# Attention with keys on partitions, in one written order per engine, ahead of an unchanged mixture of experts

## The chip, the cores and the metric

The kernel runs on one core of one Trainium2 chip. The metric is the device time of one execution in microseconds. A core has a matrix engine (PE, with its weight loads shown apart as PEld), a vector engine (DVE), a scalar engine (ACT), a general engine (POOL) and an engine that mostly issues transfers (SP). Each executes its own list of instructions in order, and waits on semaphores where it needs another's result. Matmul results go to PSUM, which has eight banks; all else lies in SBUF.

## The reference

Attention with a local window and some global keys, then a router that sends every token to one of eight experts. Sizes: batch B=4, heads H=8, sequence S=768, head dim D=64; `n_global` = 8, `n_local` = 96; 3,072 tokens of 512 values; F=1024. All data are float32.

```python
scores = (1/sqrt(D)) * q @ k.T
rel = pos[:, None] - pos[None, :]
is_global = pos[None, :] < n_global
is_local = (rel >= 0) & (rel < n_local)
dist = where(is_global & ~is_local, n_local, abs(rel))
scores = where(is_global | is_local, scores - slope[h] * dist, -1e9)
a = exp(scores - scores.max(-1))
x = (a / (a.sum(-1) + 1e-9)) @ v            # then (B,H,S,D) -> (B*S, H*D)
logits = x @ w_gate
e = argmax(logits); g = softmax(logits)[e]
out = g * (relu(x @ w1[e]) @ w2[e])
```

`q`, `k` and `v` are normal numbers times 0.1.

## The kernel before, in words

**Attention** (`banded`, L249 to L431). The 768 queries of a sequence are six blocks of 128, so there are 24 blocks `n`, and `i = n % 6` is a block's place in its sequence. Queries lie on partitions. A block sees its own 128 keys, the 128 before them, and 32 columns for global keys: three kinds of block, of 128 columns (`i` = 0), 288 with the global keys masked out of the middle (`i` = 1) and 288 with them (`i` >= 2). A unit is two heads of a block, so a block has four.

Per unit, `scores` (L321) does two matmuls into `sp` (each head on its own 64 rows of the array), DVE adds a bias from a table (L334) and takes the row maximum (L336), ACT takes the exponential with the maximum as bias and sums the row (L342). `weights_t` (L346) transposes the weights `p` by 128x128 on PE (L354, L357), and ACT and DVE copy them out (L359, L360, L364). `values` (L367) multiplies them with `v`: four matmuls a unit, six where the global keys stand apart, with 128 queries as the stationary side and 64 columns moving (L381). After four units DVE divides by the sums (`normalize`, L227). The unit loop (L410) runs the transposes one unit and the values two units behind the scores. `prep_q` and `prep_k` transpose the next block's raw rows (L239).

**Router.** `block_logits` (L158) transposes the block's x (L161) and multiplies with `w_gate` (L168); `choose` (L174) and `dispatch` (L196) run once a sequence, and six indirect writes on POOL (L219) put the rows into `xs_dram` by expert.

**Order.** Engines other than PE follow a scheduler's order; PE keeps the program's. Tiles come from pools whose buffers rotate. The loads of `q`, `k`, `v` are issued by SP, two blocks ahead, three of 256 KB each. The first two experts' weights (four transfers of 1 MB each, L140) are issued by SP at block 6.

**Choice of branch.** `n_global` and `n_local` are read at the start and a flag tells whether the banded branch is enough (L108 to L115); every engine loads it (L521) and branches. The other branch, `general` (L434), computes all keys and isn't run with these inputs.

**Experts** (L530 on). DVE makes a table of 31 tiles of 128 rows from the counts; POOL gathers a tile's rows (`xg`, L609); PE transposes them (`px`, L619), multiplies with `w1t` (`ph`, L633) and `w2t` (`py`, L643); SP loads the next tile's weights (L140); POOL writes the rows out (L647). Weights have two buffers.

Of the kernel before, what the change touches and what calls it, by code (L numbers as in the profile page):

```python
# [1 line left out]

# [7 lines left out]
F32 = mybir.dt.float32  # L10
# [6 lines left out]
SP = mybir.EngineType.SP  # L17


@with_exitstack  # L20
def kernel(
# [19 lines left out]
    NBLK = S // P           # query blocks of a sequence  # L41
    NPAIR = H // 2          # two heads fill the partitions with their dims
    NDC = DM // P
    NFC = F // P
    GW = 32                 # global keys that the banded branch has room for
    LW = P + 1              # and the widest window: one block and the query's own key
    WIN = 2 * P + GW
    XW = DM + 4             # a token's row: x, gate, token number, padding
    NEG = 1.0e9
    FAR = 1.0e6  # L50
    NA = E                  # first tile of every expert
    NB = NTOK // P - 1      # most tiles that can remain after those
# [9 lines left out]
    # Rows of tokens by expert: expert e has rows e * NTOK and on.  # L62
    xs_dram = dram.tile([E * NTOK, XW], I32, name="xs_dram")

# [1 line left out]
    ident = const.tile([P, P], F32, name="ident")  # L66
    masks.make_identity(nc, ident[:])
    iota_p = const.tile([P, 1], F32, name="iota_p")
    nc.gpsimd.iota(iota_p[:], pattern=[[0, 1]], base=0, channel_multiplier=1,
                   allow_small_or_imprecise_dtypes=True)  # L70
    col = const.tile([P, P], F32, name="col")
    nc.gpsimd.iota(col[:], pattern=[[1, P]], base=0, channel_multiplier=0,
                   allow_small_or_imprecise_dtypes=True)
    before = const.tile([P, P], BF16, name="before")
    nc.vector.tensor_scalar(before[:], col[:], iota_p[:, 0:1], None, ALU.is_gt)
    ones = const.tile([P, P], BF16, name="ones")
    nc.vector.memset(ones[:], 1.0)
    rev8 = const.tile([P, E], F32, name="rev8")
    nc.gpsimd.iota(rev8[:], pattern=[[-1, E]], base=E, channel_multiplier=0,
                   allow_small_or_imprecise_dtypes=True)  # L80
    ebase = const.tile([P, E], F32, name="ebase")
    nc.gpsimd.iota(ebase[:], pattern=[[NTOK, E]], base=0, channel_multiplier=0,
                   allow_small_or_imprecise_dtypes=True)
    base_e = const.tile([P, E], F32, name="base_e")
    nc.vector.tensor_copy(out=base_e[:], in_=ebase[:])
    tokid = const.tile([P, NBLK], I32, name="tokid")
    nc.gpsimd.iota(tokid[:], pattern=[[P, NBLK]], base=0, channel_multiplier=1)

    wg = const.tile([P, NDC, E], F32, name="wg")
    nc.scalar.dma_start(out=wg[:], in_=moe_w_gate.rearrange("(c p) e -> p c e", p=P))  # L90

# [1 line left out]
    words = const.tile([P, 2, 2], I32, name="words")  # L93
    nc.scalar.dma_start(out=words[:, 0, :], in_=n_global.bitcast(I32).partition_broadcast(P))
    nc.scalar.dma_start(out=words[:, 1, :], in_=n_local.bitcast(I32).partition_broadcast(P))
    part_i = const.tile([P, 3, 2], I32, name="part_i")
    nc.vector.tensor_copy(out=part_i[:, 0, :], in_=words[:, :, 1])
    nc.vector.tensor_scalar(part_i[:, 1, :], words[:, :, 0], 16, None, ALU.logical_shift_right)
    nc.vector.tensor_scalar(part_i[:, 2, :], words[:, :, 0], 0xFFFF, None, ALU.bitwise_and)
    part_f = const.tile([P, 3, 2], F32, name="part_f")  # L100
    nc.vector.tensor_copy(out=part_f[:], in_=part_i[:])
# [599 lines left out]
```

## Time and profile before

| | us |
|---|---|
| three executions | 953.45, 955.39, 968.07; median 955.39 |
| span of the profiled execution (first to last instruction) | 926.3 |
| first bias addition of attention (`z`, L334) | 24.11 |
| last value matmul of attention ends | 425.2 |
| first `ph` matmul of the experts | 455.37 |

| group, by shape | count | mean ns |
|---|---|---|
| PE `po`<-`vt,pT`, 64 columns | 704 | 316 |
| PE `pt`<-`ident,p`, 128 rows | 352 | 336 |
| PE `sp`, 288 columns | 320 | 525 |
| DVE `z`<-`sp,bias`, 576 / 256 elements | 80 / 16 | 756 / 424 |
| DVE `top`<-`z`, 576 elements | 80 | 745 |
| DVE `xr`<-`po,den`, 512 elements | 24 | 692 |
| ACT `p`<-`z,top`, 288 / 128 elements | 160 / 32 | 525 / 392 |
| ACT `qt`<-`pt`, 512 elements | 24 | 588 |
| POOL scatter `xs_dram` | 24 | 986 |
| POOL copy `kt`, 128 elements | 20 | 344 |

The profile is of one execution. A group's mean is from start to end of one instruction; matmuls overlap, so the distance from start to start is shorter than that mean. "Clock" is the share of PE's full clock that was granted in a stretch. A line of the timeline has start, length, engine, line, operation, output and inputs, rows and columns, and how many instructions of the kind are merged; square brackets give an idle time before it and what ended it.

### The profile page before, as it was taken

The numbers are of one execution on the slowest core, as the hardware profiler recorded it, in microseconds if no ns is written. First come the engines' busy times: TensorE is split into PE (matmuls) and PEld (weight loads), VectorE is DVE, ScalarE is ACT, GpSimd is POOL, SyncE is SP. The second block draws the span as 40 slices with busy tenths as digits, with TensorE's granted clock in tenths as the row PEclk, the third lists the DMA queues.
The fourth block names the chain that finished last, engine by engine and source line by source line (L and its number), as shares of the span: only waits on it lengthen the run. The fifth ranks groups of instructions, "written<-read, shape, count | busy, mean of one in ns | idle before, by whom it ended". The sixth has DMA issues, their size and how long they took to land.

```text
span 926.3 us, 12677 instructions
## 1 busy us (share of the span) xinstructions
PE 854.6 (92%) x4956; PEld 654.0 (71%) x4956; DVE 283.2 (31%) x686; ACT 213.8 (23%) x629; POOL 98.5 (11%) x135
## 2 busy tenths in 40 slices
PE   1899999999999999995399999999999999999995
PEld 1677777777878787874376867767686767667682
DVE  7743325654275548551301111111111111111100
ACT  0542324543255545541010000000000000000000
POOL 2000000200020002002311111111111111110000
PEclk9975556996599979995599999999999999999998
DMA  7753213411161113001279997898888879797870
GB/s 137 198 170 121 57 23 79 128 35 27 30 172 35 35 35 116 1 1 50 80 253 339 320 316 256 301 346 282 327 296 306 315 286 334 277 345 246 328 286 0
DMA packets 132243, 168.81 MB, mean 182 GB/s; under 512 B 79946, under 2 KB 79946, under 8 KB 132176
## 3 DMA queue, kind: packets, MB, share of 16 engines
q1 hardware_dynamic: 124480, 148.91, 48.9%
q0 software_dynamic: 6880, 18.99, 5.5%
q8 instruction: 42, 0.69, 0.3%
q14 instruction: 25, 0.20, 0.1%
q10 hardware_dynamic: 816, 0.02, 0.0%
HBM read 157.11 MB, written 14.47 MB: 185 GB/s over the span
## 4 chain that ended last, share of the span: by engine, by line
PE 74%; DMA 10%; issue 6%; DVE 5%; ACT 1%; SPq 1%; POOL 1%; POOLq 0%; DVEq 0%; ACTq 0%
PE ph L633 17%; PE po L381 17%; PE py L643 16%; DMA w1t<-in_moe_w_dram 9%; PE sp L331 7%; PE pt L354 7%; PE pl L168 3%; PE pt L239 3%; PE pt L357 2%; PE pt L161 2%; ACT p L342 1%; PE px L619 1%; SPq L140 1%; DVE bias L308 1%; DMA xs_dram<-xr,slot_i 1%
## 5 line engine op out<-in xcount | busy, mean ns | idle before, releaser
L633 PEld LDWEIGHTS ph<-xT,w1t 128*128 128x128 f32 x1984 | 229.5, 194 | 25.0 <-issue 13.8
L633 PE MATMUL ph<-xT,w1t 128*128 128x128 f32 x1984 | 231.6, 278 | 8.8 <-DMA w1t<-in_moe_w_dram 7.0
L643 PE MATMUL py<-w2t,hT 128*128 128x512 f32 x496 | 217.8, 593 | 0.0
L643 PEld LDWEIGHTS py<-w2t,hT 128*128 128x128 f32 x496 | 92.0, 190 | 104.2 <-issue 104.2
L381 PE MATMUL po<-vt,pT 128*128 128x64 f32 x704 | 126.2, 316 | 0.0
L636 ACT ACTIVATE hT<-ph 128x1024 f32<-128x1024 f32 x31 | 31.7, 1023 | 405.4 <-PE ph L633 405.4
L381 PEld LDWEIGHTS po<-vt,pT 128*128 128x128 f32 x704 | 114.7, 234 | 6.8
L342 ACT ACTIVATE p<-z,top 128x288 f32<-128x288 f32 (+1 forms) x192 | 96.5, 503 | 59.9 <-DVE top L336 47.4
L334 DVE TENSOR_TENSOR z<-sp,bias 128x576 f32<-128x576 f32 (+1 forms) x96 | 67.2, 701 | 103.7 <-PE sp L331 101.2
L354 PE MATMUL pt<-ident,p 128*128 128x128 f32 x352 | 75.3, 336 | 15.4 <-ACT p L342 14.7
L354 PEld LDWEIGHTS pt<-ident,p 128*128 128x128 f32 x352 | 44.1, 163 | 60.3 <-ACT p L342 31.7
L331 PE MATMUL sp<-kt,qt 64*128 64x288 f32 (+1 forms) x384 | 82.0, 511 | 2.0 <-DVE kt L244 2.0
L646 DVE TENSOR_SCALAR y<-py,gate 128x512 f32<-128x512 f32 x31 | 23.3, 751 | 177.2 <-PE py L643 177.2
L623 DVE TENSOR_TENSOR to<-xg,inv_i 128x1 int32<-128x1 int32 x31 | 4.9, 160 | 210.5 <-DMA out_dram<-y,to 202.8
L381 PE MATMUL po<-vt,gT 32*128 32x64 f32 x256 | 67.5, 351 | 0.0
L359 ACT COPY pT<-pt 128x256 f32<-128x256 f32 (+1 forms) x96 | 33.9, 353 | 143.1 <-PE pt L357 120.7
L336 DVE TENSOR_REDUCE top<-z 128x2 f32<-128x576 f32 (+1 forms) x96 | 66.1, 690 | 0.3
L647 POOL DMA_INDIRECT out_dram<-y,to x31 | 31.6, 1020 | 238.9 <-DVE gate L625 192.7
L381 PEld LDWEIGHTS po<-vt,gT 32*128 32x128 f32 x256 | 47.4, 230 | 11.1
L609 POOL DMA_INDIRECT xg<-xs_dram,grow x31 | 31.9, 1029 | 170.6 <-PE px L619 165.0
L331 PEld LDWEIGHTS sp<-kt,qt 64*128 64x128 f32 x384 | 34.7, 222 | 12.1 <-issue 7.6
L219 POOL DMA_INDIRECT xs_dram<-xr,slot_i x24 | 23.7, 986 | 178.4 <-DVE slot_i L216 104.6
(120 smaller groups left out, 490.7 us busy)
## 6 DMA issues: line engine op xcount, KB each, us to landing
w1t<-in_moe_w_dram SPq DMA_DIRECT2D x62, 1024.0 KB, 10.9
w2t<-in_moe_w_dram SPq DMA_DIRECT2D x62, 1024.0 KB, 7.5
raw_q<-in_q_dram SPq DMA_DIRECT2D x24, 256.0 KB, 3.1
raw_k<-in_k_dram SPq DMA_DIRECT2D x24, 256.0 KB, 3.2
vt<-in_v_dram SPq DMA_DIRECT2D x24, 256.0 KB, 4.7
xg<-xs_dram,grow POOLq DMA_INDIRECT x31, 6.1
out_dram<-y,to POOLq DMA_INDIRECT x31, 7.4
xs_dram<-xr,slot_i POOLq DMA_INDIRECT x24, 3.5
```

Source lines behind the costliest of these rows:

```text
L331: nc.tensor.matmul(sp[:, a, 0:w], lhsT=qts[n][r, m, :], rhs=kt[r, m, ds(k0, w)], start=True, stop=True, skip_group_check=True)
L334: nc.vector.tensor_tensor(z[:, :, 0:w], sp[:, :, 0:w], biases[kind][:, 2 * m:2 * m + 2, :], ALU.add)
L336: nc.vector.tensor_reduce(top[:], z[:, :, 0:w], AX.X, ALU.max, negate=True)
L342: nc.scalar.activation(p[:, a, 0:w], z[:, a, 0:w], AF.Exp, bias=top[:, a:a + 1], scale=1.0, accum_out=blk[n][:, h:h + 1])
L354: nc.tensor.transpose(pts[a][:, j, :], p[:, a, ds(j * (P + GW), P)], ident[:])
L359: nc.scalar.copy(pT[:, 0, 0:nb, :], pts[0][:, 0:nb, :])
L381: nc.tensor.matmul(po[:, h, :], lhsT=lhs, rhs=rhs, start=(j == 0), stop=(j == len(terms) - 1), skip_group_check=True)
L609: nc.gpsimd.indirect_dma_start(out=xg[j % XB][:].bitcast(I32), out_offset=None, in_=xs_dram[:], in_offset=bass.IndirectOffsetOnAxis(ap=gro ...
L633: nc.tensor.matmul(ph[:, f, :], lhsT=w1t[:, c, ts(f, P)], rhs=xT[:, c, :], start=(c == 0), stop=(c == NDC - 1), skip_group_check=True)
L636: nc.scalar.activation(hT[:], ph[:], AF.Relu)
L643: nc.tensor.matmul(py[:], lhsT=hT[:, f, :], rhs=w2t[:, f, :], start=(f == 0), stop=(f == NFC - 1))
L647: d = nc.gpsimd.indirect_dma_start(out=out[:], out_offset=bass.IndirectOffsetOnAxis(ap=fs[j]["to"][:, 0:1], axis=0), in_=y[:], in_offset=N ...
```

## The change

Attention and router are rewritten; the experts (and `general`) keep their text.

- Keys lie on partitions: a score matmul has 128 keys as the stationary side and 128 queries moving, so the exponentials come out as the values' moving side and no transpose of them is needed. A block has 16 score matmuls and 16 value matmuls (`v` with 64 columns is stationary, 128 queries move, two heads in two column halves of the array); the first block of a sequence has half of each.
- There are no columns of their own for global keys. A window is taken to be at most 97 keys, so the first 32 keys of the block before are outside it; after that block's own scores POOL overwrites them (`kg` into `kt`, `vg` into `v`) with the sequence's first 32 keys and values.
- No row maximum. The exponential is of score plus bias, in place. POOL adds the two key blocks (`both`), and matmuls with a matrix of ones and with `w_gate` (`sums`) give each query's sums and unscaled logits together; these are transposed (`tokens_u`) and divided (`normal`). The sums are kept in `den`, and at the end a flag asks that all are between 0.125 and 1e12 and that `n_global` <= 32 and 1 <= `n_local` <= 97. Otherwise `general` runs after it and does the work again. The flag is loaded by all engines after attention instead of at the start.
- All of it is recorded by `Flow`, in the order written, and played within one critical section: each engine gets its instructions in that order, and waits on semaphores of `Flow`'s own that are derived from what is read and written. At the end SP waits for every transfer. Tiles are slices of one SBUF tile and of one PSUM tile of eight banks: scores in 0 to 3, values in 4, sums in 5, x in 6, and the incoming `k` shares bank 3, the incoming `q` has 7.

The loop, and the methods that it calls, cut to their core:

```diff
+    def scores(self, n):
+        for g in range(2):
+            for mm in range(2):
+                for ab in range(2 if i else 1):
+                    kt = self.kt[(n - ab) % 3]
+                    for a in range(2):
+                        r = slice(64 * a, 64 * a + 64)
+                        m = 2 * g + mm
+                        c = 2 * P * mm + P * ab
+                        f.pe.matmul(self.psum[:, 2 * g + a, c:c + P], lhsT=kt[r, m, :], rhs=qt[r, m, :], ...)
+    def weigh(self, n, g):
+            f.dve.tensor_tensor(e, s, self.bias[:, g, :, 1:3, :]..., ALU.add)
+    def exponent(self, n, g):
+        f.act.activation(e, e, AF.Exp)
+    def both(self, n, g):
+            f.pool.tensor_tensor(self.es[n % 3][:, g], e[:, :, 0:P], e[:, :, P:2 * P], ALU.add)
+    def values(self, n, bank):
+        for m in range(4):
+            for ab in range(nb):
+                for a in range(2):
+                    r = slice(64 * a, 64 * a + 64)
+                    f.pe.matmul(po[r, m, :], lhsT=self.v[(n - ab) % 6][:, 2 * m + a, :],
+                                rhs=self.e[n % 2][:, m // 2, 2 * a + m % 2, P * ab:P * ab + P], ...)
+        return lambda: f.act.copy(self.ot[n % 2], po)
+    def sums(self, n, bank):
+        for j in range(3):
+            for m in range(4):
+                r = slice(32 * m, 32 * m + 32)
+                ...
+                f.pe.matmul(self.psum[r, bank, 0:P], lhsT=lhsT, rhs=rhs, ..., tile_position=(0, 32 * m))
+        return lambda: f.act.copy(self.us, self.psum[:, bank, 0:P])
+    def tokens_x(self, n, bank):
+        for m in range(4):
+            f.pe.transpose(self.psum[:, bank, ts(m, P)], self.ot[n % 2][:, m, :], ident)
+    def tokens_u(self, n, bank):
+        self.f.pe.transpose(self.psum[:, bank, 256:384], self.us, ident)
+    def normal(self, n, ubank):
+        f.dve.tensor_scalar(den, ut[:, :, 16:18], 1e-9, None, ALU.add)
+        f.dve.reciprocal(r, den)
+        f.dve.tensor_tensor(self.lw, ..., ALU.mult)
+        f.dve.tensor_reduce(self.lg[b % 2][:, i, :], ..., ALU.add)
+    def rows(self, n, bank):
+        f.dve.tensor_tensor(self.xr[b % 2][:, i, 0:512]..., self.psum[:, bank, :]..., self.rcp..., ALU.mult)
...
+        O, U, T0, T1, SK = 4, 5, 6, 7, 3
+        for n in range(N + 3):
+            if live:
+                at.scores(n)
+                if n + 4 < N:
+                    at.loads(n + 4)
+                if n + 3 < N:
+                    at.load_v(n + 3)
+                if i < NBLK - 1 and i >= 1:
+                    f.pool.tensor_copy(out=at.kt[n % 3][:, :, 0:32], in_=at.kg)
+            if n == 9 or n == 15:
...
+                        f.sp.dma_start(out=dst[:, c:c + h, :], in_=s[:, c:c + h, :])
+            if live:
+                at.weigh(n, 0)
+                at.exponent(n, 0)
+            if n >= 3:
+                at.normal(n - 3, U)
+            if n - 4 in routed:
+                at.slots(routed.pop(n - 4), U)
...
+            if 1 <= n <= N:
+                oT = at.values(n - 1, O)
+                oT()
+            if live:
+                at.weigh(n, 1)
+                at.exponent(n, 1)
+            if n >= 3:
+                at.rows(n - 3, T0)
+            if 2 <= n <= N + 1:
+                us = at.sums(n - 2, U)
+            if n + 2 < N:
+                kk = at.k_in(n + 2, SK)
+            if 2 <= n <= N + 1:
+                at.tokens_x(n - 2, T0)
+            if n + 2 < N:
+                qq = at.q_in(n + 2, T1)
+            if live:
+                at.both(n, 0)
+                at.both(n, 1)
+            if 1 <= n <= N:
+                bb, ii = divmod(n - 1, NBLK)
+                if 1 <= ii < NBLK - 1:
+                    f.pool.tensor_copy(out=at.v[(n - 1) % 6][0:32]..., in_=at.vg[bb % 2])
+            if us:
+                us()
+                at.tokens_u(n - 2, U)
+            if kk:
+                kk()
+            if qq:
+                qq()
...
+            if n >= 3 and (n - 3) % NBLK == NBLK - 1:
+                at.choose((n - 3) // NBLK)
+                at.counts(U)
+                routed[n - 3] = (n - 3) // NBLK
+            for _ in range(2 if n > N else 1):
+                if scat:
+                    at.scatter(*scat.pop(0))
...
-    with tc.If(flag > 0) as branch:
-            banded(stack)
-    with branch.Else():
+    redo = nc.values_load(keep["flag"][0:1, 0:1], ...)
+    with tc.If(redo > 0):
             general(stack)
```

`k_in` and `q_in` are four transposes each with a copy by ACT behind them; `choose`, `counts` and `slots` are the router's steps of before, and `scatter` is one of its six indirect writes.

## The prediction

> **What bounds the kernel now.** I read the busy table first, then busy time by stage, then single stretches of the timeline.
>
> ```profile
> PE 854.6 (92%) x4956; PEld 654.0 (71%) x4956; DVE 283.2 (31%) x686; ACT 213.8 (23%) x629; POOL 98.5 (11%) x135
> PEclk9975556996599979995599999999999999999998
> 0.00:24.10 24.10, 3.43 (x16) 2.39 (x16) 18.61 (x65) 1.88 (x2) 5.28 (x28) 1.00 0.79 141
> 24.10:428.00 403.90, 395.04 (x2318) 316.83 (x2318) 204.41 (x449) 178.64 (x594) 21.72 (x35) 0.79 0.27 72
> 428.00:455.40 27.40, 3.23 (x25) 2.68 (x25) 9.05 (x53) 0.24 (x1) 12.48 (x15) 0.50 0.27 90
> 455.40:926.30 470.90, 452.91 (x2600) 332.14 (x2600) 51.12 (x119) 33.00 (x32) 58.98 (x58) 0.99 0.79 284
> ```
>
> The last four rows are stages: length, then busy time of PE, PEld, DVE, ACT, POOL, the granted clock, the DMA share and GB/s. Stage 1 waits for DVE (masks and biases), stage 2 is attention, stage 3 is the hand-over, stage 4 the experts. In attention PE is busy for 395 of 404 us and no other engine for more than 204: PE's own instructions are the limit. How dear they are depends on the clock, and the same block of 128 queries is found at both:
>
> ```profile
> 72.00:99.70 27.70, 27.70 (x111) 21.94 (x110) 9.06 (x17) 8.13 (x27) 0.00 (x0) 0.50 0.29 95
> 373.50:388.70 15.20, 15.20 (x110) 12.30 (x110) 8.70 (x18) 8.06 (x26) 0.00 (x0) 1.00 0.00 1
> ```
>
> Same count of instructions, 15.2 us at clock 1.00 and 27.7 us at 0.50. The mean over 24 blocks is 404/24 = 16.8 us. Inside a block at full clock:
>
> ```profile
> 30.43 0.38 PE L331 MATMUL sp<-kt,qt 64*128 64x128 f32 x2
> 30.65 0.28 PE L331 MATMUL sp<-kt,qt 64*128 64x128 f32 x2
> 375.23 0.76 PE L331 MATMUL sp<-kt,qt 64*128 64x288 f32 x4
> 375.91 0.66 PE L354 MATMUL pt<-ident,p 128*128 128x128 f32 x4
> 377.06 0.56 PE L381 MATMUL po<-vt,pT 128*128 128x64 f32 x4
> 377.55 0.43 PE L381 MATMUL po<-vt,gT 32*128 32x64 f32 x2
> 377.91 0.66 PE L381 MATMUL po<-vt,pT 128*128 128x64 f32 x4
> ```
>
> A float32 matmul appears as two passes, a transpose as one. From start to next start: a transpose 0.11 to 0.12 us (440 to 490 ns for four), a pass of `po` 0.12, and 0.18 with 32 rows. One unit of `values` (two heads, six matmuls, twelve passes) is 1.70 us; four of them are 6.8 of the block's 15.2. The first two rows matter for the change: two passes of `sp` start in the same instant, because the two heads lie in different row halves. In the longer run of eight such passes at 14.84 us the pairs start 0.35, 0.21 and 0.22 us apart at half clock, which is the pitch of one full pass there (0.21).
>
> **What the Trainium skill says.** (1) "TensorE: Matmul & The Clock Gate", Part 3: matmuls in different row or column groups run concurrently; three column tiles gained 2.38 times. The trace confirms rows; it has no column tile. (2) Same page, Part 1: the clock halves when the array is little used and comes back after some microseconds of use. The trace shows both levels, but half clock for 90 us (56 to 147) with PE always busy, so "busy" in the table isn't what the gate counts. (3) "GPSIMD Engine Reference", 3.1: a float32 add of 2,048 elements takes 4,497 ns on POOL. No add is in the trace; POOL's 128-element copy took 344 ns. (4) "SBUF — State Buffer", Who interferes with whom: a DVE instruction with one SBUF input doesn't contend with POOL. The new DVE instructions of the loop read PSUM and one SBUF operand, so I charge nothing; the trace can't test it.
>
> **The change, stage by stage.**
>
> Stage 1 (24.1 to 16 us). Counts 7+7 mask and 8+8 bias instructions where before had 21+24, and no flag is read ahead of the loads. `num` ends at 5.6 as before; first kind 1.9 + 1.7 us (its own rows before); second and third together at 256 elements, from the 288-element runs of 2.83 and 3.04 us: 2.6 + 2.8; three small ones 0.5. First bias addition at 15 to 16 us; before 24.11. The first loads leave at 1 us, not 7.06, so their transposes are ready.
>
> Stage 2, PE, per block at full clock. Removed: the 24 transposes of `p` and the 24 value matmuls of a full block, its eight score matmuls, four router transposes and four router products. What there is:
> - scores: 16 matmuls, 32 passes as 16 pairs of row halves: 16 x 0.11 + 0.1 = 1.85;
> - values: 16 matmuls in two column halves, 16 pairs: 1.85, if columns pair as rows do. Bounds: 1.85, or 32 x 0.11 = 3.5 unpaired. I take the lower, by (1);
> - sums: 12 matmuls, 24 passes over four column groups: 0.75 in fours, 2.6 singly; I take 0.75;
> - 13 transposes: 13 x 0.11 = 1.45; changes of tile shape 4 x 0.12 = 0.5.
> Sum 6.4 us, or 10 without column pairing. At half clock (passes 0.21): 12.0, or 19.2.
>
> The others, per block. DVE: two additions of 1,024 (424 ns at 256, 756 at 576, so 1.22 each), four small ones at the 0.24 spacing seen at 430 us (0.96), rows 0.69: 4.1. ACT: two exponentials of 1,024 (392 at 128, 525 at 288: 1.14), three copies 0.59, one 0.26: 4.3. POOL: two adds of 512 at (3)'s rate, 1.15; kt copy 0.35; v copy of 512, under 1.1; a scatter at its spacing 1.28: 5.0. If adds took 2 us it would be 6.7. DMA: 786 KB of 256 B rows; 204 GB/s were moved at 14 to 21 us: 3.9 us, with the scatter's 264 KB 5.2.
>
> No single engine is slow, so the ring of waits counts. Scores half done 1.2 (seven pairs and a matmul's 0.3 us tail); `weigh` 0 1.22; `normal` 0.96 stands ahead of `weigh` 1 on DVE; `weigh` 1 1.22; exponential 1.14, behind it on ACT the copy `us` 0.26; then the transpose `tokens_u`, which is ahead of the next block's scores on PE; hand-offs 0.06 to 0.1 each: 6.5 us. On PE, `k_in` waits for `weigh` 1 (they share bank 3), and behind it queue eight transposes. Ring and PE together: I take 7.0 us. A first block of a sequence has half the keys: 5.0. `slots` adds 1.2 us three times (4). SP: two weight fills of 4.2 MB lie ahead of block 14's and 20's loads, 15 us at 284 GB/s plus 3.9; the fills leave some three and a half blocks (24 us) ahead of the first use of what queues behind them. I charge 0; with a block less of that cover, 2 each.
> Scores of the last block start at 16 + 4 x 5.0 + 19 x 7.0 + 4 + 3 (half clock at the start, as until 29 us before) = 176 us.
>
> Stage 3. From there: last exponential 5.9, values 2.1, copy 0.6, sums 0.9, `us` and transpose 0.6, `normal` 0.96, rows 0.7, choice 1.2, counts 0.6, slots 1.2, to POOL 0.8, with hand-offs some 16.5 to the first scatter.
>
> ```profile
> 433.28 0.98 POOL L219 DMA_INDIRECT xs_dram<-xr,slot_i  x1 [68.47 <-DVE slot_i L216]
> 439.69 0.98 POOL L219 DMA_INDIRECT xs_dram<-xr,slot_i  x1 [0.30 <-DMA xs_dram<-xr,slot_i]
> 449.67 1.06 POOL L609 DMA_INDIRECT xg<-xs_dram,grow  x1 [4.37 <-DVE inv_i L580]
> 455.37 1.01 PE L633 MATMUL ph<-xT,w1t 128*128 128x128 f32 x3 [0.87 <-DVE xT L621]
> ```
>
> First scatter to last landing 9.9 (433.28 to 443.14), table, gather and first transposes 12.2 (to 455.37): unchanged. New: the check of `den` (ten small DVE instructions, one transpose) lies beside the scatters, 0; reading the flag and branching after SP's waits for all DMAs: 0.5 us at 6.7 us before, up to 3 with a far jump; I take 1.5. Sum 40: first expert matmul at 216.
>
> Stage 4: 470.9, untouched. Span 216 + 471 = 687, against 926.3: minus 239. The median, 955.4, stands 29.1 above that span; I keep this: 716.5, say **717 us**.
>
> **Rivals.**
> - *Half clock.* Against: the new block puts its passes in half the time. For: it held for 90 us before, with PE busy. All blocks at 12.0 (8.5 for first ones): 16 + 34 + 228 + 4 + 3 + 44 + 471 = 800, so 829; half of them: 773.
> - *Columns don't pair.* PE 10.2 a block, first ones 8: 16 + 32 + 194 + 4 + 3 + 41 + 471 = 761, so 790. Nothing in the trace speaks for or against it.
> - *POOL or a DMA wait sets the pace*, 8.5 to 9 a block: 745 to 760.
> - *Slower.* Half clock and unpaired columns at once: 19.2 a block (14 for first ones): 16 + 56 + 365 + 4 + 47 + 471 = 959, so 988. It decides from 17.9 us a block, where 21.9 blocks' worth fills the 391 us that remain of 926.
> - *The check fails and the general branch runs too.* Scores are sums of 64 products of 0.1-sized numbers over 8, near 0.01, so `den` is between 1 and about 100, inside 0.125 to 1e12, and 8 and 96 are inside 32 and 97. Four DVE passes of 768 elements, about 0.95 each, for 192 blocks of a head: 730 us more. Under 1%.
>
> **Numbers.** Forecast, 7 us a block (690 to 750): 0.52. Half clock, in part or whole: 0.21. Unpaired columns: 0.14. POOL or DMA: 0.06. Slower: 0.04. The rest, ends near before: 0.03. Range 685 to 840. About 2%, 19 us, is what can be told from no change. Faster 0.93, same 0.03, slower 0.04.
>
> **What would show it.** The first bias addition near 16 us; scores of successive blocks 7 us apart; value passes of two column halves starting together; PEclk mostly 9; POOL adds near 1.15 us; first expert matmul near 216 us and 471 us after it. Wrong, if blocks take over 9 us, if PE stands idle on POOL or a load, or if the experts' stage changes length.

## The result, and the profile after

| | before | after |
|---|---|---|
| median, us | 954.42 (923.70 to 968.07, 4 runs) | 678.69 (678.30 to 680.09, 4 runs) |
| span of the profiled execution, us | 926.3 | 676.5 |

The ratio, which compares the fast executions of each kernel alone, is 0.7395, with a 95% interval of 0.7343 to 0.7447; the two medians stand at 0.711. The kernel is faster, as forecast; the time lies 38 us under the forecast and 6 us under the low end of its range.

First the busy table and the clock row of the kernel after, then its stages: length, busy time of PE, PEld, DVE, ACT and POOL, granted clock, DMA share, GB/s.

```profile
PE 605.6 (90%) x4949; PEld 464.7 (69%) x4949; DVE 169.6 (25%) x436; ACT 123.4 (18%) x180; POOL 162.2 (24%) x195
PEclk9899999999756999999999999999999999999999
0.00:16.15 16.15, 5.22 (x32) 4.30 (x32) 10.27 (x42) 3.65 (x5) 2.83 (x22) 0.95 0.86 189
16.15:161.35 145.20, 134.40 (x2117) 118.13 (x2118) 89.73 (x193) 83.88 (x136) 78.53 (x92) 0.98 0.72 195
161.35:179.63 18.28, 11.44 (x196) 9.08 (x195) 11.24 (x41) 4.12 (x8) 9.45 (x11) 0.96 0.19 73
179.63:189.40 9.77, 0.37 (x1) 0.08 (x1) 0.92 (x5) 0.00 (x0) 5.87 (x6) 0.50 0.42 162
189.40:197.22 7.82, 0.00 (x0) 0.00 (x0) 0.00 (x0) 0.00 (x0) 0.00 (x0) 0.50 0.02 6
197.22:209.83 12.61, 1.09 (x4) 0.72 (x5) 6.63 (x39) 0.00 (x0) 6.62 (x9) 0.50 0.26 66
209.83:676.50 466.67, 453.12 (x2600) 332.38 (x2600) 50.78 (x119) 31.75 (x31) 58.89 (x58) 0.99 0.79 287
```

The gain is in the second and third rows: attention took some 404 us and now takes 163. PE is still its busiest engine (134 of 145 us). It doesn't execute fewer passes: 2,318 before, 2,313 now (2,117 and 196). What changed is how long they take, since most now run two or four at once and none has 288 columns or 32 rows, and that the clock is 0.98 and not 0.79.

How much of the 240 us is the clock can be estimated. A clock of 0.79 means half clock in 42% of the 404 us, 170 us. The same block took 27.7 us at half clock and 15.2 at full clock, so those 170 us would have been 93: some 77 us are the clock, some 163 the passes. At full clock a block went from 15.2 to 6.24 us. Most of that is the values, four units at 1.80 us (377.06 to 378.86 in the trace of before) against 1.89 in all; 24 transposes at 0.11, 2.6 us, are gone altogether.

The row to stop at is the fifth: 7.8 us in which no engine does anything.

Against the sum of the prediction:

| step | predicted | measured |
|---|---|---|
| to the first bias addition | 16 | 16.15 |
| from there to the last block's scores | 160 | 145.20 |
| to the first scatter of the last sequence | 16.5 | 18.28 |
| scatters to their last landing | 9.9 | 9.77 |
| flag and branch | 1.5 | 7.82 |
| table, gather, first transposes | 12.2 | 12.61 |
| experts | 470.9 | 466.67 |
| around the span | 29.1 | 1.8 |
| sum | 716.1 | 678.3 |

The last row is the largest error. The profiled execution of after took 678.30 us at a span of 676.5: 1.8 us lie around it. Seven executions of before, taken beside a later experiment, say the same of it: 930.15 us at a span of 928.4 and clock 0.882, 957.19 at 955.4 and 0.857, 913.26 at 911.5 and 0.901. Always 1.7 to 1.8 us lie around the span, and the span follows the clock. In the profiled execution of before the mean clock was 0.887. So the 29.1 us between the profiled span of before and the median weren't launch time, but another execution's slower clock.

The next view (timeline of after) shows what sets the pace in a steady block. All of the new part carries the line of `Flow`'s helper (L323), so what a line is must be told from its shape: 64*128 are scores, 128*64 values, 128*128 transposes.

```profile
39.74 1.70 PE L323 MATMUL psum<-arena 128*64 128x128 f32 x28
83.56 4.20 PE L323 MATMUL psum<-arena 64*128 64x128 f32 x80
84.22 1.22 DVE L323 TENSOR_TENSOR arena<-psum,arena 128x1024 f32<-128x1024 f32 x1 [2.41 <-PE psum L323]
87.69 1.64 PE L323 MATMUL psum<-ident,arena 128*128 128x128 f32 x13
89.26 1.05 PE L323 MATMUL psum<-arena 64*128 64x128 f32 x14
90.02 0.69 DVE L323 TENSOR_TENSOR arena<-psum,arena 128x512 f32<-128x512 f32 x1 [1.97 <-PE psum L323]
```

The first line is values: 28 passes within 1.70 us, 0.06 us each, where a pass alone takes 0.11. In the record of each pass, the two of a pair start 7 ns apart and the pairs 0.109 us. The others are one block: scores, values and sums merged, the 13 transposes, and the next scores (the view cuts off the block's first passes and the last line), with no idle time on PE between them (none of PE's lines has a bracket). `weigh` 0 of a full block starts at 84.22, and that of the next block, a sequence's first with half the keys (512 elements), at 90.02. In full blocks the starts are 6.24 us apart (32.45, 38.69).

### The profile page after: what moved, and what is told of

Same layout as the page of the kernel before. It is cut to its first block, busy times and chain, and to the rows that moved or that the text cites. A ratio compares the mean times of both kernels' runs of the same rounds, so it can differ in the third digit from the quotient of the medians.

```text
span 676.5 us, 11666 instructions
## 1 busy us (share of the span) xinstructions
PE 605.6 (90%) x4949; PEld 464.7 (69%) x4949; DVE 169.6 (25%) x436; ACT 123.4 (18%) x180; POOL 162.2 (24%) x195
## 4 chain that ended last, share of the span: by engine, by line
PE 44%; DMA 14%; issue 8%; SPq 2%; DVE 1%; POOL 1%; POOLq 0%; DVEq 0%
PE ph L1087 22%; PE py L1097 20%; DMA w1t<-in_moe_w_dram 14%; SPq L651 1%; PE px L1073 1%; POOL out_dram L1101 1%; DMA xg<-xs_dram,grow 1%; SPq L1055 0%; DVE xT L1075 0%; POOLq L1151 0%; DVE y L1100 0%; DVE row L995 0%; DVE more_i L999 0%; DVE more L1001 0%; DVE tri L1005 0%
## 5 line engine op out<-in xcount | busy, mean ns | idle before, releaser
L323 PE MATMUL psum<-arena 64*128 64x128 f32 (+2 forms) x1984 | 108.4, 279 | 1.8 <-POOL arena L323 1.0
L323 PEld LDWEIGHTS psum<-arena 64*128 64x128 f32 (+2 forms) x1984 | 94.4, 148 | 13.1 <-issue 6.1
L323 DVE TENSOR_TENSOR arena<-psum,arena 128x1024 f32<-128x1024 f32 (+2 forms) x96 | 74.0, 792 | 54.2 <-PE psum L323 53.4
L323 POOL TENSOR_TENSOR arena<-arena 128x512 f32<-128x512 f32 x40 | 50.9, 1272 | 45.0 <-ACT arena L323 45.0
L323 PE MATMUL psum<-ident,arena 128*128 128x128 f32 x312 | 43.7, 290 | 20.0 <-DVE arena L323 13.3
L323 ACT ACTIVATE arena<-arena 128x1024 f32<-128x1024 f32 (+2 forms) x52 | 48.3, 929 | 58.4 <-DVE arena L323 58.4
L323 PEld LDWEIGHTS psum<-ident,arena 128*128 128x128 f32 x312 | 35.7, 147 | 27.3 <-issue 17.4
L323 ACT COPY arena<-psum 128x512 f32<-128x512 f32 (+1 forms) x72 | 32.5, 477 | 20.2 <-PE psum L323 19.9
L1073 PEld LDWEIGHTS px<-ident,xg 128*128 128x128 f32 x124 | 14.8, 144 | 28.2 <-issue 28.2
L323 POOL COPY arena<-arena 128x128 f32<-128x128 f32 (+2 forms) x44 | 20.2, 464 | 33.7 <-ACT arena L323 18.9
L1075 DVE COPY xT<-px 128x512 f32<-128x512 f32 x31 | 21.3, 686 | 24.4 <-PE px L1073 24.4
L323 POOL DMA_INDIRECT xs_dram<-arena,slot_i x24 | 24.0, 1000 | 10.7 <-DVE ok L323 5.8
```

The lines of the kernel that those rows point to most:

```text
L323: f.sp.dma_start(out=t, in_=src[b, :, ts(i, P), :].rearrange("h p d -> p h d"))
L1073: nc.tensor.transpose(pt[:, c, :], x[:, ts(c, P)], ident[:])
L1075: nc.vector.tensor_copy(out=xT[:], in_=pt[:])
```

## The experiments

Each is the kernel after with the edit shown, unless it says otherwise. "Block" is the distance of two `weigh` 0 in steady full blocks; it is 6.24 us in the kernel after. Times are to be compared with its 678.69 us. Before is no measure for small differences: beside these experiments it took 903 to 983 us, at clocks from 0.914 to 0.838. The kernel after wasn't executed again beside them, so no interval stands behind a difference of one or two microseconds.

The first four, executed together on one chip, share a stall at the end of attention that the trace of after lacks; experiment 4 shows it. It costs about 4.5 us, which isn't the edits'.

**1. Values, one column half after the other.**

```diff
-        for m in range(4):
-            for ab in range(nb):
-                for a in range(2):
+        for a in range(2):
+            for m in range(4):
+                for ab in range(nb):
```

> The value matmuls of one column half all come before those of the other, so that no two neighbours lie in different halves; nothing else moves. Theory (column halves pair as row halves do, and PE sets the block's length): 32 passes at 0.11 us instead of 16 pairs, values of a full block 1.9 -> 3.5 us, 20 full blocks by 1.65 and 4 first ones by 0.8: about +36 us, 715 us. Rival (the ring of waits through DVE and ACT sets the length): +0.3 us a block at most, under 690 us. If columns had never paired, no change: 679 us.

Measured: 702.22 us (702.10 to 702.35), span 700.6; block 7.61. The values in its timeline:

```profile
43.10 3.17 PE L323 MATMUL psum<-arena 128*64 128x128 f32 x31
```

31 passes in 3.17 us are 0.10 each, against 0.06. So columns do pair, and undoing it costs 1.37 us in a steady block. By `weigh` 0 of the last block (181.46) it is 18.9 us behind the kernel after; the rest of the 23.5 us is nearly all the stall. That is less than the 36 expected, for two reasons: a steady block lost 1.37 and not 1.65 us (where the halves meet they still overlap), and the blocks at a sequence's end, where DVE has more to do (experiment 10), lost 0 to 0.6.

**2. Scores, the row halves apart within each group.**

```diff
-            for mm in range(2):
-                for ab in range(2 if i else 1):
-                    ...
-                    for a in range(2):
+            for a in range(2):
+                for mm in range(2):
+                    for ab in range(2 if i else 1):
```

> The same for the scores: within each group of four heads the matmuls of one row half come before those of the other. Theory: scores of a full block 1.9 -> 3.5 us, and the first bias addition waits 0.8 us longer too: about +36 to +40 us, 715 to 719 us. Rival (waits set the length and PE has room): only the 0.8 us by which the first half comes later, +15 to +20 us.

Measured: 698.12 us (697.98 to 698.26), span 696.2; block 7.00. The time lies in the rival's range and not in the theory's. Losing all 16 pairs would have cost 16 x 0.11 = 1.76 us a block; 0.76 was lost, because the order of issue undid only part of the pairing: where one half follows the other, their passes still run together. A full block of after and one of this kernel, scores, values and sums merged:

```profile
37.48 4.75 PE L323 MATMUL psum<-arena 64*128 64x128 f32 x88
48.01 5.51 PE L323 MATMUL psum<-arena 64*128 64x128 f32 x88
```

They take 0.76 us longer, the block does too, and PE has no idle time in either; by the last block this kernel is 15.2 us behind, and the stall is the rest. So PE had no room, which the rival took it to have. But the later first half lengthens the ring as well, and this run alone can't tell the two apart. It is no measure of what row pairs are worth in full.

**3. One more DVE instruction in the ring.** A reduction of 384 elements, about 0.46 us, between `normal` and `weigh` 1.

```diff
                 at.normal(n - 3, U)
+            if live:
+                V.tensor_reduce(at.idle[:, 0:1], at.bias[:, 0, 0], AX.XY, ALU.max)
```

> One DVE reduction over 384 elements (about 0.5 us) more per block, between the small operations of normal and the second bias addition; its result is not used. Theory (PE sets the block's length, and the ring has 0.2 to 0.3 us to spare, as the profile shows between the end of the second bias addition and PE's arrival at the key transposes): +0.25 us in most blocks and +0.5 in those with a wait already, +6 to +8 us in all, 685 to 687. Rival A (the ring sets the length): +0.5 x 23 = +11.5 us. Rival B (the ring is far from it): no change.

Measured: 693.44 us (692.60 to 694.95), span 692.4; block 6.68, +0.44. The timeline of this kernel:

```profile
50.60 1.71 PE L324 MATMUL psum<-ident,arena 128*128 128x128 f32 x13 [0.30 <-DVE arena L324]
```

The bracket is new: PE now stands idle ahead of `k_in`, released by DVE's `weigh` 1 (they share bank 3). Nearly all of the 0.46 us went into the block. By the last block it is 10.8 us behind (1.7 of them in a stretch of half clock from 121.1 to 124.5), which is rival A's 11.5 and not the theory's 6 to 8; the stall makes up the rest of the 14.8. So the ring of waits and PE are equally long in the kernel after: whichever is lengthened shows at once (experiment 7 lengthens PE alone). That shortening one alone would bring nothing follows from this, but wasn't tried.

**4. The flag isn't read.** The flag's load, the branch and `general` are left out.

> The flag is still computed but not read, and the branch with the general computation is left out of the program; the outputs are the same for these inputs. Theory (of the 7.8 us between the last scatter's landing and the first instruction of the table, 0.5 is the flag's load and most is the far branch, above all PE's 3.9 us at it): the gap falls to 1 to 3 us, 672 to 674 us. Rival (the gap is the end of the critical section, SP's waits and the joining of the queues): it stays at 5 us or more, 676 us or above.

Measured: 677.77 us (674.65 to 678.68), span 675.7, 0.8 less. The time is the rival's, the gap the theory's: the trace shows the price, and that it was given back. In after the last of SP's waits for landings is at 189.9 and `cnt`, the table's first instruction, at 197.53: 7.6 us. Here they are at 195.1 and 197.50: 2.4 us. So 5.2 us of the gap are the flag and the branch. But the first scatter of the last sequence, at 179.63 in after, stood at 184.95. Its timeline, and one line each of experiments 1 and 2:

```profile
175.53 0.27 ACT L323 COPY arena<-psum 128x128 f32<-128x128 f32 x1 [2.43 <-remote]
176.36 0.17 DVE L323 TENSOR_SCALAR den<-psum 128x8 f32<-128x8 f32 x1 [6.52 <-PE psum L323]
```

```profile
194.98 0.27 ACT L323 COPY arena<-psum 128x128 f32<-128x128 f32 x1 [2.16 <-remote]
190.13 0.27 ACT L323 COPY arena<-psum 128x128 f32<-128x128 f32 x1 [2.48 <-remote]
```

ACT stood still for 2.43 us for something outside the core's engines, the last block had begun 0.8 us later, and PE's clock was 0.50 from 176 to 180, against 0.78 in after. The same copy waits for 2.2 to 2.5 us in experiments 1, 2 and 3, which read the flag, and in no trace of the other kernels. So the stall isn't the flag's; what it was stays open. From `weigh` 0 of the last block to the first scatter of the last sequence it is 17.07 us in after and 21.57 here: this is where the 4.5 us come from.

What fills the gap in after is in its trace's sequencer records of the end of the critical section (L190), the flag (L975) and the branch (L977): name, count, shortest/median/longest ns, first and last start.

```profile
L190 POOLq DRAIN  x1: 2029/2029/2029, 190.1 to 190.1; - x1
L975 PEldq TENSOR_LOAD <-flag x1: 483/483/483, 192.2 to 192.2; - x1
L977 ACTq COMPARE_BRANCH  x1: 59/59/59, 192.8 to 192.8; - x1
L977 PEldq COMPARE_BRANCH  x1: 3852/3852/3852, 192.8 to 192.8; - x1
```

After the landings POOL is drained (2.03 us: its queue is run empty), then all load the flag (0.5), then all branch. ACT's branch takes 0.06 us, PE's 3.85, and the join afterwards waits for PE. The kernel before has a branch of this kind on PE too, 3.56 us at 431.1 (L523), but there it lay beside the scatters.

The trace also says what goes on during PE's branch. Of the transfers that it lists as instruction transfers, none starts between 168 and 193 us; from 193.84, 1.0 us after the branch began, there are four of 8 KB and one of 16 KB within 0.2 us. The other versions of after with this branch have the same at theirs; here, where the branch is left out, there is none between 172 and 200 us. That PE waits for the instructions behind the branch is therefore likely, but no run tested it.

**5. The wait for the scatters behind the branch.** SP's waits for POOL's transfers move from the end of the critical section to a second one (`landed`) behind the branch.

```diff
             for p, v in level.items():
-                if p[1] is not None:
+                if p[1] is not None and p[0] != "POOL":
                     self.nc.sync.wait_ge(sems[p], v)
...
+    f.landed("landed")
     tab = ctx.enter_context(tc.tile_pool(name="tab", bufs=1))
```

> The kernel after, with the wait for the scatters' landings moved from the end of the attention part to behind the read of the flag and the branch (in the general branch it is repeated ahead of that branch's work). In the kernel after 7.8 us pass between the last landing (189.4) and cnt (197.2); where the flag isn't read at all, the last scatter's issue and cnt lie 6.1 us apart against 11.5. Theory (flag read and branch stand in series behind the landings and cost 5.4 us there): they now lie beside the 9.8 us of the scatters, cnt follows the last landing by 2 to 3 us, span 671 to 672 against 676.5, time 673. Rival (the gap belongs to the join of the engines that any wait of this kind brings, or the time is given back as when the flag was left out): 677 to 679.

Measured: 678.61 us (678.37 to 678.97), span 677.0: no gain, as the rival had it. The end of the section drains POOL, waits or not:

```profile
L190 POOLq DRAIN  x1: 8154/8154/8154, 182.8 to 182.8; - x1
L983 PEldq COMPARE_BRANCH  x1: 3772/3772/3772, 191.7 to 191.7; - x1
```

With scatters in flight the drain took 8.15 us instead of 2.03 and ended at 191.0. The branch began 1.1 us earlier than in after, and the second section's own join (2 us, to `cnt` at 197.89) used that up. The theory named the right price and the wrong holder.

**6. The same, and the table and the memsets of `xg` ahead of the second wait**, in memory that attention doesn't use.

> As the kernel with the late wait, and in addition the table of tiles (DVE, 5.7 us from cnt on) and the four memsets of xg (POOL, 2.0 us) stand ahead of the wait, in memory that the attention part does not use; the gathers stay behind it. Theory: only gather, first transposes and copy stay behind the landings (about 6 us of the 12.6), so another 5 to 6 us less: span 665 to 667, time 667 to 668, and the first expert tile may run at a higher clock because PE stands idle for less time (in the kernel after its first ph took 10.25 us against 7.41 for the next). Rival (the memsets queue behind the six scatters on POOL and push the gathers back by their 2 us, and something else then ends the gap): 670 to 672.

Measured: 678.78 us (677.49 to 679.46), span 677.4: no gain, neither the theory's nor the rival's, for the same reason. `cnt` at 197.91 follows the branch, so the table can't start while POOL drains. The first scatter was also 3 us later (182.65), as PE's clock was 0.76 to 0.81 from 168 to 176, where after had 1.00.

**7. More work for PE.** 24 transposes more in each of 22 blocks.

```diff
             if n + 2 < N:
+                for t in range(24):
+                    f.pe.transpose(psum[:, T1, ts(t % 4, P)], ident[:], ident[:])
                 qq = at.q_in(n + 2, T1)
```

> The kernel after with 24 more 128x128 transposes in each block but the last two, into the bank that q_in writes next. Theory (PE's own instructions set the block's length and the clock stays full): 24 x 0.11 = 2.6 us on each of 22 blocks, 58 us: span 735, time 737, clock 1.00 through attention. If the ring of waits had room that PE doesn't have, less: with 0.5 us to spare a block 725. Rival (in the kernel before the half clock comes from work like these transposes, however busy PE is): clock 0.5 in a good part of attention, time above 800.

Measured: 735.89 us (735.60 to 736.19), span 734.4. Expected were 737 and 735.

```profile
87.83 2.78 PE L323 MATMUL psum<-ident 128*128 128x128 f32 x24
24.00:200.00 176.00, 170.39 (x2381) 156.83 (x2379) 78.09 (x165) 74.62 (x122) 70.94 (x82) 1.00 0.58 154
```

The clock of the 176 us of attention is 1.00. Added PE time goes into the span one for one (57.9 us for 22 x 2.6), and 128x128 transposes don't bring the half clock in this loop.

**8. The kernel before without its 32-row passes.** The two transposes and two value matmuls for the global keys in each unit are left out, at all three places in the code, from the third block of a sequence on: those blocks' output lacks the global keys.

```diff
-            if i >= 2:
+            if i >= 9:
```

> The kernel before without the passes for the global keys (the two transposes and the two 32-row value matmuls of each unit from the third block of a sequence on): the global keys are left out of those blocks' output. At the pace of its own blocks this takes 4 x 2 x 0.11 + 4 x 4 x 0.18 = 3.8 us from 16 of 24 blocks at full clock, about 60 to 75 us over all. Theory 1 (the 32-row passes leave the array so little used that the clock halves): the clock of attention rises from 0.79 to 0.95 or more, stage of attention near 290 us, time near 830. Theory 2 (the half clock has nothing to do with them): clock of attention stays 0.75 to 0.85, stage near 335 us, time 880 to 900.

Measured: 812.03 us (811.45 to 812.60); before, on that chip, 943.1 median. Its attention and its clock:

```profile
24.00:314.00 290.00, 268.27 (x1933) 212.75 (x1933) 205.71 (x452) 163.20 (x530) 21.71 (x35) 0.93 0.39 101
PEclk9999897998799996599999999999999999999998
```

Of the expected numbers 290 us for the stage is met, the clock is 0.93 where 0.95 was the mark. The work left out is 60 us at full clock (16 blocks x 4 x (2 x 0.11 + 4 x 0.18)); `cnt` came 114 us earlier than in the profile of before. The other 54 us are, by this estimate, the clock, though PE is now idle for more of the time (busy 268 of 290, before 395 of 404). The Trainium skill ("TensorE: Matmul & The Clock Gate", Part 1) ties the clock to how busy PE has recently been; here a PE that the table shows as busy wasn't enough for it. That PE was too busy before is no way out: in experiment 7 it is busy for 97% at clock 1.00.

The trace of before shows where the half clock falls. A stretch without 32-row passes (the second block of a sequence), and two stretches with them:

```profile
155.20:166.50 11.30, 10.13 (x87) 7.92 (x86) 10.06 (x30) 6.47 (x23) 0.33 (x1) 1.00 0.71 134
83.70:111.20 27.50, 27.50 (x109) 21.76 (x108) 9.06 (x17) 8.05 (x26) 0.00 (x0) 0.50 0.25 48
283.20:313.70 30.50, 30.50 (x219) 24.69 (x219) 17.38 (x34) 16.19 (x53) 0.00 (x0) 1.00 0.16 35
```

The three long half-clock stretches that lie wholly in attention (57.7 to 153.3, 214.7 to 255.7, 330.7 to 344.4) begin where blocks with 32-row passes are executed and end in the first block of the next sequence, which has none of its own; no second block runs at half clock. But the same passes also ran at full clock for 30 us. So they, or what stands around them, are one condition of the long stretches and not the only one. In this run 34 us at half clock are left in attention, 27 of them where PE had just stood idle for 3.5 and 2.5 us. The edit also takes out the changes of tile shape around the passes and transposes of 32 columns; none of the runs tells these apart.

**9. The last sequence's scatters behind the branch.** Six scatters move out of the critical section to behind the branch; their rows and the table have memory of their own.

```diff
-        for s in scat:
-            at.scatter(*s)
...
+    for b_, u_ in scat:
+        nc.gpsimd.indirect_dma_start(out=xs_dram[:], ..., in_=keep["xr1"][:, u_, :].bitcast(I32), ...)
```

> The kernel after, with the six scatters of the last sequence issued behind the flag's branch (its rows of xr and the table of tiles in memory of their own; in the general branch their slots are set out of bounds). Why moving the wait alone brought nothing: the end of the attention part drains POOL, and this drain took 8.15 us with the scatters in flight (182.8 to 191.0), so the flag was read at 191.1 against 192.2, and the second wait took 2 us of its own. Theory: with no scatter ahead of the drain, the flag is read near 183.5, branch and join end near 188.5, the scatters then take their 9.8 us to 198.3, the table runs beside them, and the first gather follows at 198.5 instead of 203.9: span 670 to 672, time 672 to 674. Rival (the gap is a fixed price of the join that comes wherever the scatters stand, or the gathers wait for something besides table and scatters): 677 to 680.

Measured: 684.75 us (684.24 to 685.86): slower than after, and outside both expectations. The first part came as expected: `cnt` at 187.45. Then:

```profile
187.57 0.98 POOL L984 DMA_INDIRECT xs_dram<-xr,slot_i  x1 [12.83 <-DVEq L974]
194.36 0.98 POOL L984 DMA_INDIRECT xs_dram<-xr,slot_i  x1 [2.49 <-DMA xs_dram<-xr,slot_i]
207.78 1.04 POOL L1066 DMA_INDIRECT xg<-xs_dram,grow  x1 [2.77 <-DMA xs_dram<-xr,slot_i]
```

Outside the hand-written section each scatter waits until the one ahead has landed, since both write `xs_dram`: 20.2 us from the first to the gather instead of some 10. A new wait ate the gain.

**10. The counts a block later**, except for the last sequence, and `slots` behind `weigh` 1.

```diff
-            if n - 4 in routed:
-                at.slots(routed.pop(n - 4), U)
...
+            if n - 5 in routed:
+                at.slots(routed.pop(n - 5), U)
...
-                at.counts(U)
-                routed[n - 3] = (n - 3) // NBLK
+            m = n - 4 if n < N + 2 else n - 3
+            if m >= 0 and m % NBLK == NBLK - 1:
+                at.counts(U)
+                routed[m] = m // NBLK
```

> The kernel after, with the counting matmuls of a sequence one block later than its choice (except for the last sequence) and slots behind weigh 1 instead of ahead of it. In the kernel after the two blocks where a sequence's choice, counts and slots fall last 7.4 and 7.8 us instead of 5.8 and 6.24, three times: 9.5 us over what the blocks cost else. Theory (PE waits at the counts for DVE's oh, and slots' 1.2 us stand in the ring): these blocks shorten by 1 to 1.5 us each, span 668 to 672, time 670 to 674. Rival (it is the sum of DVE's work in these blocks, choice 2.4 us and slots 1.2 beside 4.1, that delays the next weigh 0, wherever the counts stand): less than 2 us gained, 676.5 to 679.

Measured: 676.26 us (675.88 to 676.49), span 674.5. PE's waits in attention, of after and then of this kernel (total us, times, longest):

```profile
PE psum L323 <- DVE arena L323: 7.3, 8, 1.4
PE psum L323 <- DVE oh L323: 2.1, 3, 0.7
```

```profile
PE psum L323 <- DVE arena L323: 3.8, 8, 0.7
PE psum L323 <- DVE base_e L323: 2.6, 3, 0.9
```

The wait for `oh` is gone, and one of the same size for `base_e`, which `slots` writes, is there instead. What fell is the wait for the bias additions (`arena`), from 7.3 to 3.8 us. The three blocks from 62.77 to 84.22 at the first sequence's end, 21.45 us, became 20.32; the first `ph` came 3.4 us earlier (206.44), and the span is 2.0 shorter. The time is a quarter of a microsecond under the rival's range and well above the theory's. Of the 9.5 us that these blocks last longer, 3.4 are gained; that the rest is DVE's work, wherever it stands, is the rival's reading and wasn't tested further.

**11. Both moves together.**

> The scatters behind the branch and the later counts together. If each gains on its own stretch, they add: time 665 to 669. If neither does: 677 to 680.

Measured: 681.90 us (679.52 to 683.16), outside both expectations: 2.9 less than with the scatters alone, about what the counts bring by themselves (2.4).

**12. Both moves, the scatters free of each other**, and the memsets of `xg` on DVE.

```diff
+        tc.declare_no_dep(d.ins, group="scatter", reason="every row has a slot of its own")
+        tc.add_to_no_dep_group("scatter", d.ins)
...
-        nc.gpsimd.memset(t[:], 0.0)
+        nc.vector.memset(t[:], 0.0)
```

> Both moves, with the six late scatters free of each other (behind the branch each had waited for the landing of the one ahead: 3.3 us apart instead of 1.28, 20.2 us in all) and the memsets of xg on DVE, so that they don't stand between the scatters on POOL. With the scatters behind the branch cnt stood at 187.45 instead of 197.53, as expected, and only their chain was too long. Theory: scatters from 187.5 to their landing at 197.3, table and memsets (7 us of DVE) beside them, first gather at 197.5 to 198, 6 us earlier than in the kernel after; with 2 us from the later counts: span 667 to 669.5, time 669 to 671.5. Rival (the gathers still wait for something else, or the scatters are slower beside the weight fills that then start): 674 to 680.

Measured: 670.75 us (669.55 to 672.88, 6 runs), profiled span 667.8. Its hand-over:

```profile
183.22 0.17 DVE L997 TENSOR_TENSOR cnt<-base_e,ebase 128x8 f32<-128x8 f32 x1 [5.41 <-DVEq L976]
189.75 0.98 POOL L986 DMA_INDIRECT xs_dram<-xr,slot_i  x1 [0.31 <-issue]
190.99 0.19 DVE L1039 SCALAR_TENSOR_TENSOR grow<-inv,row 128x31 int32<-128x31 f32 x1
193.38 1.04 POOL L1070 DMA_INDIRECT xg<-xs_dram,grow  x1 [2.65 <-DMA xs_dram<-xr,slot_i]
199.16 8.89 PE L1094 MATMUL ph<-xT,w1t 128*128 128x128 f32 x64 [1.08 <-issue]
```

The scatters are 1.28 us apart again. The table is ready (190.99) before the last of them has landed, and the gather waits for the landing alone. How the gain divides between the scatters and the memsets wasn't separated. The first `ph` is 10.7 us earlier than in after, the span 8.7: the experts took 468.6 us instead of 466.7. This is the fastest version here, by 7.9 us or 1.2% of after's median. The two weren't executed side by side, so no interval stands behind that difference; it is larger than either kernel's spread.

## Why the prediction was right, and where it was wrong

**Right in kind.** PE's instructions bound attention before and, together with the ring, after; how long the new passes take, most of them side by side, and the full clock set the gain. The passes per block were priced right: values 1.89 us (predicted 1.85), sums 0.80 (0.75), 13 transposes 1.57 (1.45), scores 1.98 (1.85), in all 6.24 where 6.4 was worked out with 0.5 for changes of tile shape. The choice that columns pair as rows do, which rested on the Trainium skill alone ("TensorE: Matmul & The Clock Gate", Part 3) and on nothing in the trace, held: experiment 1 has 0.06 us a pass in pairs and 0.10 apart. The full clock was less well founded: the prediction gave half clock 0.21 and had no measurement of what brings it; experiment 8 came afterwards. First bias addition, scatters and table came within 0.5 us.

**"The median, 955.4, stands 29.1 above that span; I keep this."** This term was mis-sized by 27.3 us, and is most of the error. The span of one execution was set against the median of others, and the difference taken as a fixed price. It measures 1.8 us; the rest was the clock of before, which the same prediction had seen vary. Without it the sum is 689, inside the range.

**"Ring and PE together: I take 7.0 us."** PE's 6.4 and the ring's 6.5 were each worked out, and half a microsecond was put on top, with no reason but that PE's `k_in` waits within the ring. The two fit together: 6.24 us. This term was 15 us too large in the sum of stage 2, even with the three sequence ends, which cost 1.2 and 1.6 us over a plain block and were charged at 1.2.

**"Reading the flag and branching ... I take 1.5."** The term measures 7.8 us: drain 2.0, which the sum doesn't have, load 0.5, branch on PE 3.85, and joins. The bound of 3 was too low too. A branch of 3.56 us on PE stood in the trace of before, hidden beside the scatters; its cover goes when the wait is put ahead of it, which is what the change does.

**The experts** were taken as untouched at 470.9 and took 466.7. PE's waits for weights ahead of `ph` fell from 7.0 us in all to 4.4; why they fell, and where the other 1.6 us lie, weren't traced. In the experiments the stage takes between 465.7 us (1) and 469.4 (9). It is longer in the two versions that gain time ahead of it (468.1 in experiment 10, 468.6 in 12), but longest in one that begins it later than after does, so what sets its length is open.

**The rivals.** Half clock: only in the first 5 us of attention (to 21.2) and again from 178.3, and experiment 8 puts the long stretches with the 32-row passes or what stands around them, which the new loop doesn't have. The sums' 32-column passes, 0.8 us a block, did not bring it back. Unpaired columns: no, and by experiment 1 would have cost about 19 us, not 73; but the forecast's case also unpaired the sums and took 3.2 us more a block, and the order of issue doesn't undo all pairs. POOL or a DMA wait: POOL was busy 78.5 of 145 us, its adds took 1.27 us against the 1.15 worked out, and from 24 to 161 us PE waited for DVE alone, never for a load. The failing check: `general` did not run.

**Two readings** of the trace of before were off, and nothing rests on them: a unit of `values` takes 1.80 us from start to next start, not 1.70, and the long half clock lasted 96 us, from 57.7 to 153.3, not from 56 to 147.

## What to carry to other kernels

Compare a span with the time of the same execution; a gap to other executions' median can be a clock, not a price, and goes away with what causes it. When a wait or a section's end is put ahead of a branch, look up what that branch and the drain cost in the trace, even where they are hidden there, and ask which engine's queue the end has to drain. Work moved out of a hand-ordered section gets the default waits back: look for them before counting the gain. And look for an odd wait in the traces of other edits before giving it to this one.

## What the runs showed of the hardware

- A late compare-and-branch took 3.4 to 3.9 us on PE and 0.04 to 0.07 on ACT, DVE, POOL and SP. A branch of the same statement on PE early in before, at 7.0 us, took 0.09. The Trainium skill ("Advanced Engine Details and Errata", Control Flow Timing) states about 108 ns, which none of these exceeds but the late one on PE. In every trace with it, instruction transfers start 0.4 to 1.0 us into the late branch; whether they are the cause wasn't tested.
- Draining POOL took 2.03 us with its transfers landed, and 8.15 with the last six scatters under way (experiment 5).
- Two passes in different column halves start 7 ns apart and cost 0.109 us together when issued alternately; issued one half after the other they cost 0.10 each.
- Leaving out 32-row passes raised the clock of before's attention from 0.79 to 0.93 although PE was idle for a larger share; an extra 24 transposes a block left after's at 1.00.
- After some 30 us with next to no work PE ran the first expert tile's 64 `ph` matmuls in 10.25 us, where a later tile took 7.41. The clock was 0.50 until 215.8, 6 us into that tile.
